# Output product of two gated linear-attention blocks: eight half-size products made seven

## The chip, the cores and the metric

The kernel runs on one core of a Trainium2 chip. The metric is device time in microseconds (us) from one launch; lower is better. Three runs of the kernel before gave 212.53, 211.25 and 210.63 us, a median of 211.25 us. In the views, PE is TensorE's matmul side and PEld its weight load, DVE is VectorE, ACT ScalarE, POOL GpSimd, SP SyncE; a `q` after an engine (SPq) means DMA issues from that engine's queue.

## The reference

Two linear-attention blocks A and B read the same x (2048 rows, 640 columns, bf16). Each has 32 heads of 20 columns, and they are mixed by a gate per row:

```python
def _A_ref(x, wqkv, wo):                      # _B_ref is the same
    qkv = (x @ wqkv) ...                      # q, k, v: 32 heads of 20
    phi = lambda t: jnp.where(t > 0, t + 1, jnp.exp(t)) + 1e-6
    pq, pk = phi(q), phi(k)
    kv = jnp.einsum("bhsd,bhse->bhde", pk, v)
    z = jnp.einsum("bhsd->bhd", pk)
    num = jnp.einsum("bhqd,bhde->bhqe", pq, kv)
    den = jnp.einsum("bhqd,bhd->bhq", pq, z)[..., None] + 1e-6
    return merged_heads(num / den) @ wo
x = A_x
g = _sigmoid((x * gate_w).sum(-1, keepdims=True))
return g * a + (1 - g) * b
```

## The kernel before, in words

Everything is kept transposed so that no activation has to be turned over. For each block b the kernel makes `pqT[b]`, the 640 features of phi(q) on partitions (five chunks `c` of 128) by 2048 rows, scaled in place by gate and 1/den; and `M[b]`, a 640 x 640 matrix that holds kv and wo folded together. The output is then one product over both blocks: out = pqT[A]^T M[A] + pqT[B]^T M[B].

The stages, in the order of the program, are these.

- `k_first` and `k_chunk` (lines 174 to 189): k for 16 row tiles of 128, ten matmuls of 320 columns each; `phi` (166 to 172) is an exp on ScalarE and two instructions on VectorE.
- `q_pass` (386): q in ten units of 1024 columns, with the row sums `z_rows` (235) between the first two. VectorE's `zr` (246) is what the sums go through.
- `g_all` (398): five passes `g_pass` of 32 matmuls (x^T phi(k) for one feature chunk), copied to `GT` by ScalarE (`evac`, 217 to 220). Between them `norm_unit` (312) scales `pqT[b]`.
- `kvt_pass` (263): 30 short matmuls into one PSUM tile, then six masked copies on VectorE into `KVT` (280).
- `m_unit` (287): four matmuls for 128 rows of `M[b]`, then a copy by `evac`.
- The output stage. Row tile i needs 20 matmuls of 320 columns: 2 blocks x 2 column halves x 5 chunks. Tiles 0 and 1 are woven into block B's `kvt_pass` and `m_unit` through `final_mm` (332), so that TensorE has work while `GT`, `KVT` and `M[B]` are copied. Tiles 2 to 14 go through `final_group` (348), tile 15 through `final_last` (360), which splits its columns 448 and 192 so that the last copy and the last DMA are small. Each tile is copied to bf16 by ScalarE or VectorE in turn (`final_out`, 344) and written to memory by SP's queue.

Block B runs after block A; A's `M` units sit among B's k chunks.

Order and waits: a scheduler orders each engine's instructions and adds the semaphore waits. PSUM is eight banks of 512 fp32 columns; `ps` (57) hands out four tiles (slots 0 to 3), each of two banks. Waits are made per tile and not per bank: a writer of one bank of a tile waits for earlier readers of the other bank of that tile.

The block that the change replaces is at lines 450 to 471:

```python
    for c in range(DT):
        m_unit(1, c, ("act", "dve")[c % 2], 1 + c % 2)
        if c > 0:
            for i in range(2):
                final_mm(i, 1, c - 1, pts[i])
```

Of the kernel before, what the change touches and what calls it, by code (L numbers as in the profile page):

```python
# [20 lines left out]
HB = 512  # L21
HF = D // 2
JW = 120
NJ = 6
EPS = 1e-6
RB = 256


@with_exitstack
def kernel(  # L30
# [11 lines left out]
    nc = tc.nc  # L42
# [35 lines left out]
    gwr = persist.tile([P, DT, H], BF16, name="gwr")  # L78
    zero = persist.tile([P, HB], BF16, name="zero")
    grow = persist.tile([1, D], BF16, name="grow")  # L80
    ge = [persist.tile([P, 2 * RB], FP32, name=f"ge{b}") for b in "AB"]

    wq_dram = [A_wqkv.rearrange("(c p) f -> p c f", p=P), B_wqkv.rearrange("(c p) f -> p c f", p=P)]
# [25 lines left out]
    for r in range(4):  # L109
        rows = slice(32 * r, 32 * r + 32)  # L110
# [8 lines left out]
    for r in range(4):  # L119
        rows = slice(32 * r, 32 * r + 32)  # L120
# [96 lines left out]
    def evac(dst, pt, eng):  # L217

        copy = nc.scalar.copy if eng == "act" else nc.vector.tensor_copy
        copy(out=dst.rearrange("p (b n) -> p b n", b=2), in_=pt[:, :, 0:HF])  # L220
# [42 lines left out]
    def kvt_pass(b, slot=None):  # L263

        pt = ps(f"kv{'AB'[b]}", slot)
        for j in range(NJ):
            e0 = JW * j if j < NJ - 1 else D - P
            d0 = JW * j
            w = min(JW, D - d0)
            dst = pt[:, j // 3, (j % 3) * JW:(j % 3) * JW + w]  # L270
            for c in range(DT):
                nc.tensor.matmul(
                    dst, lhsT=wv[b][:, c, e0:e0 + P], rhs=GT[:, c, d0:d0 + w], start=(c == 0), stop=(c == DT - 1),
                )
        for j in range(NJ):
            last = j == NJ - 1
            rows = P if last else JW
            nh = 2 if last else 6
            mask = maskE[:rows, DT - 1, H - 2:H] if last else maskE[:rows, 0, 0:6]
            nc.vector.tensor_tensor(  # L280
                out=KVT[:rows, j, JW * j:JW * j + nh * Dh].rearrange("p (h t) -> p h t", t=Dh),
                in0=pt[:rows, j // 3, (j % 3) * JW:(j % 3) * JW + nh * Dh].rearrange("p (h t) -> p h t", t=Dh),
                in1=mask[:, :, None].to_broadcast([rows, nh, Dh]),
                op=ALU.mult,
            )

    def m_unit(b, c, eng, slot=None):

        pt = ps(f"m{'AB'[b]}", slot)
        for hf in range(2):  # L290
            for k, j in enumerate((c, c + 1)):
                rows = P if j == NJ - 1 else JW
                nc.tensor.matmul(  # L293
                    pt[:, hf, 0:HF], lhsT=KVT[:rows, j, c * P:(c + 1) * P],
                    rhs=wo_sb[b][:rows, j, hf * HF:(hf + 1) * HF], start=(k == 0), stop=(k == 1),
                )
        evac(M[b][:, c, :], pt, eng)

    def rec_pass(b, h, zsel, slot):
# [9 lines left out]
            nc.vector.reciprocal(out=rT[:], in_=d1[:])  # L309
        return rT  # L310

    def norm_unit(b, h, rT, ms, slots):

        pts = [ps(f"ex{'AB'[b]}", s) for s in slots]
        for k, m in enumerate(ms):
            for j in range(4):
                nc.tensor.matmul(
                    pts[j // 2][:, j % 2, k * RB:(k + 1) * RB], lhsT=E4[32 * j:32 * j + 32, m * P:(m + 1) * P],
                    rhs=rT[32 * j:32 * j + 32, :], start=True, stop=True,
                )  # L320
        n = len(ms)
        for jj in range(2):
            src = pts[jj][:, :, 0:n * RB].rearrange("p j (m n) -> p j m n", n=RB)
            r0 = h * 2 * HB + jj * HB
            dst = pqT[b][:, ms[0]:ms[0] + n, r0:r0 + HB].rearrange("p m (j n) -> p j m n", n=RB)
            if jj == 1:
                ex = work.tile([P, 2, n, RB], BF16, tag=f"ex{n}", name="ex")
                nc.scalar.copy(out=ex[:], in_=src)
                src = ex[:]
            nc.vector.tensor_tensor(out=dst, in0=src, in1=dst, op=ALU.mult)  # L330

    def final_mm(i, b, c, pt):
        for hf in range(2):
            nc.tensor.matmul(  # L334
                pt[:, hf, 0:HF], lhsT=pqT[b][:, c, i * P:(i + 1) * P], rhs=M[b][:, c, hf * HF:(hf + 1) * HF],
                start=(b == 0 and c == 0), stop=(b == 1 and c == DT - 1),
            )

    def rows_of(i):
        n, q = divmod(i, CB)  # L340
        rows = out2[n * HB:(n + 1) * HB, :]
        return rows.rearrange("(p q) d -> q p d", q=CB)[q] if n == 0 else rows[q * P:(q + 1) * P, :]

    def final_out(i, pt):
        osb = work.tile([P, D], BF16, tag="osb", name="osb", bufs=3)
        evac(osb[:], pt, ("act", "dve")[i % 2])
        nc.sync.dma_start(out=rows_of(i), in_=osb[:])

    def final_group(i):
        pt = ps("o")  # L350
        for hf in range(2):
            for b in range(2):
                for c in range(DT):
                    nc.tensor.matmul(  # L354
                        pt[:, hf, 0:HF], lhsT=pqT[b][:, c, i * P:(i + 1) * P], rhs=M[b][:, c, hf * HF:(hf + 1) * HF],
                        start=(b == 0 and c == 0), stop=(b == 1 and c == DT - 1),
                    )
        final_out(i, pt)

    def final_last(i):  # L360

        osb = work.tile([P, D], BF16, tag="osb", name="osb", bufs=3)
        for lo, hi, copy, eng in ((0, 448, nc.vector.tensor_copy, nc.sync), (448, D, nc.scalar.copy, nc.scalar)):
            pt = ps("o")
            for k in range(2 * DT):
                b, c = divmod(k, DT)
                nc.tensor.matmul(  # L367
                    pt[:, 0, 0:hi - lo], lhsT=pqT[b][:, c, i * P:(i + 1) * P], rhs=M[b][:, c, lo:hi],
                    start=(k == 0), stop=(k == 2 * DT - 1),
                )  # L370
            copy(out=osb[:, lo:hi], in_=pt[:, 0, 0:hi - lo])
            eng.dma_start(out=rows_of(i)[:, lo:hi], in_=osb[:, lo:hi])

    def load_w(b, which, eng):
        lo = {"q": 0, "k": D, "v": 2 * D}[which]
# [22 lines left out]
    def g_all(b, zsel):  # L398

        units = [(h, ms) for h in range(2) for ms in ((0, 1), (2, 3), (4,))]  # L400
        rts = [rec_pass(b, 0, zsel, 0)]

        def norm():
            h, ms = units.pop(0)
            norm_unit(b, h, rts[h], ms, (2, 3))

        g_pass(b, 0, 1, lambda: rts.append(rec_pass(b, 1, zsel, 2)))
        for c in range(1, DT):
            if c > 1:
# [21 lines left out]
    zsel = q_pass(0)  # L431
    wq[1] = load_w(1, "q", nc.sync)
    g_all(0, zsel)


    turn[0] = 2
# [5 lines left out]
    for i in range(3, ST):  # L442
        k_chunk(1, i)
        if i % 2 == 0 and i // 2 - 2 < DT:
            m_unit(0, i // 2 - 2, "act")
    zsel = q_pass(1)
    g_all(1, zsel)


    pts = [ps("o", 0)]  # L450
    for c in range(DT):
        final_mm(0, 0, c, pts[0])
    kvt_pass(1, 2)
    pts.append(ps("o", 3))
    for c in range(DT):
        final_mm(1, 0, c, pts[1])
    for c in range(DT):
        m_unit(1, c, ("act", "dve")[c % 2], 1 + c % 2)
        if c > 0:
            for i in range(2):  # L460
                final_mm(i, 1, c - 1, pts[i])
    for i in range(2):
        final_mm(i, 1, DT - 1, pts[i])
        final_out(i, pts[i])
    for i, slot in ((2, 1), (3, 2), (4, 0), (5, 3)):
        turn[0] = slot
        final_group(i)
    for i in range(6, ST - 1):
        turn[0] = (1, 2, 0, 3)[(i - 2) % 4]
        final_group(i)  # L470
    final_last(ST - 1)


# [28 lines left out]
```

## Time and profile before

| what | value |
|---|---|
| runs before | 210.63, 211.25, 212.53 us |
| span of the profiled execution (the page gives no other time for it) | 209.1 us |
| TensorE busy | 200.8 us, 96% |
| VectorE, ScalarE busy | 113.7 us (54%), 74.2 us (35%) |
| granted TensorE clock, mean | 1.000 |
| block B's last g matmul is followed by the output stage's first at | 157.69 us |
| last DMA issue (ScalarE's queue, 48 KB) | 206.44 us |

The span runs from the first to the last instruction. A matmul's duration in a row (299 ns for 320 columns) is its way through the array; matmuls overlap, and the distance from start to start is what each costs a busy TensorE. In a timeline line the first two numbers are start and length, and the bracket at the end says how long the engine sat idle before it and what ended that.

### The profile page before, as it was taken

The page shows a single profiled execution, that of the slowest core. Times are in us where ns is not written, and L with a number is a line of the kernel's source. Part 1 is how long each engine was busy: PE and PEld are TensorE (multiplying, and loading weights), DVE is VectorE, ACT ScalarE, POOL GpSimd, SP SyncE. Part 2 cuts the span into 40 slices and gives each one's busy share as a digit, 9 for nine tenths or more (in the row PEclk, how much of TensorE's full clock was granted, in tenths as well). Part 3 has the DMA queues.
Part 4 walks back from the last instruction along what each step waited for, and adds up shares of the span by engine and source line. Part 5 has one row for each costly group of instructions (what it writes and reads, how often), then busy time and mean ns, then how long its engine had stood idle before and what let it go on. Part 6 is the DMA issues. An engine that isn't in the chain of part 4 may idle for free.

```text
span 209.1 us, 3659 instructions
## 1 busy us (share of the span) xinstructions
PE 200.8 (96%) x1561; PEld 126.6 (61%) x1567; DVE 113.7 (54%) x170; ACT 74.2 (35%) x96; POOL 8.6 (4%) x22
## 2 busy tenths in 40 slices
PE   7996989999999999999999999999999999999994
PEld 3674665444466667777764444566667677777762
DVE  3396665867895571677676677957542311111111
ACT  2452545253503452356653435225431331111110
POOL 8800000000000000000000000000000000000000
PEclk9999999999999999999999999999999999999999
DMA  6664499992050000130000000000000011111111
GB/s 202 181 78 101 100 299 365 230 223 94 2 157 3 0 0 3 18 138 3 0 0 3 0 0 0 5 0 0 3 0 3 0 63 67 62 63 63 66 63 63
DMA packets 18015, 14.21 MB, mean 68 GB/s; under 512 B 8863, under 2 KB 17744, under 8 KB 18000
## 3 DMA queue, kind: packets, MB, share of 16 engines
q1 hardware_dynamic: 17422, 13.45, 23.3%
q10 hardware_dynamic: 578, 0.54, 0.8%
q8 instruction: 12, 0.20, 0.4%
q14 instruction: 3, 0.02, 0.0%
HBM read 9.40 MB, written 2.62 MB: 58 GB/s over the span
## 4 chain that ended last, share of the span: by engine, by line
PE 82%; SPq 9%; DMA 3%; DVE 2%; ACT 1%; issue 1%; DVEq 0%; ACTq 0%
PE o L354 17%; PE gB L229 11%; PE gA L229 11%; PE kB L175 10%; PE qA L211 9%; PE qB L211 9%; SPq L103 9%; PE o L334 3%; PE kA L175 2%; DMA wkA<-in_A_wqkv_dram 2%; DMA xT<-in_A_x_dram 1%; PE mA L293 1%; PE o L367 1%; PE mB L293 1%; ACT e L170 1%
## 5 line engine op out<-in xcount | busy, mean ns | idle before, releaser
L175 PEld LDWEIGHTS <-xT 128*128 128x128 bf16 x320 | 30.8, 98 | 15.9 <-DMA xT<-in_A_x_dram 3.4
L229 PEld LDWEIGHTS <-xn 128*128 128x128 bf16 x320 | 29.8, 98 | 14.0 <-issue 2.5
L171 DVE TENSOR_SCALAR e<-e 128x640 bf16<-128x640 bf16 (+1 forms) x52 | 19.4, 374 | 24.6 <-ACT e L170 22.9
L175 PE MATMUL kA<-wkA,xT 128*128 128x320 bf16 x160 | 22.9, 299 | 2.8 <-DMA xT<-in_A_x_dram 2.6
L229 PE MATMUL gB<-pk,xn 128*128 128x320 bf16 x160 | 23.3, 300 | 0.0
L229 PE MATMUL gA<-pk,xn 128*128 128x320 bf16 x160 | 23.3, 300 | 0.0
L175 PE MATMUL kB<-wkB,xT 128*128 128x320 bf16 x160 | 22.9, 299 | 0.0
L354 PE MATMUL o<-MA,pqTA 128*128 128x320 bf16 x130 | 22.1, 299 | 0.0
L354 PE MATMUL o<-MB,pqTB 128*128 128x320 bf16 x130 | 21.9, 299 | 0.0
L211 PE MATMUL qA<-xT,wqA 128*128 128x512 bf16 x97 | 21.8, 379 | 0.1
L211 PE MATMUL qB<-xT,wqB 128*128 128x512 bf16 x97 | 21.8, 379 | 0.1
L220 DVE CAST osb<-o 128x640 bf16<-128x640 f32 x7 | 5.8, 824 | 29.2 <-PE o L354 27.4
L211 PEld LDWEIGHTS <-wqB 128*128 128x128 bf16 x100 | 9.6, 98 | 11.4 <-issue 0.3
L220 ACT CAST osb<-o 128x640 bf16<-128x640 f32 x8 | 5.5, 692 | 31.0 <-PE o L354 30.5
L211 PEld LDWEIGHTS <-wqA 128*128 128x128 bf16 x100 | 9.5, 97 | 11.6 <-issue 0.5
L170 ACT ACTIVATE e<-kA 128x640 bf16<-128x640 f32 x16 | 11.3, 706 | 14.5 <-PE kA L175 14.5
L354 PEld LDWEIGHTS <-pqTB 128*128 128x128 bf16 x130 | 12.7, 98 | 4.9
L354 PEld LDWEIGHTS <-pqTA 128*128 128x128 bf16 x130 | 12.7, 98 | 4.9
L170 ACT ACTIVATE e<-kB 128x640 bf16<-128x640 f32 x16 | 11.3, 704 | 11.7 <-PE kB L175 11.7
L170 ACT ACTIVATE e<-qB 128x1024 bf16<-128x1024 f32 x10 | 10.2, 1024 | 13.4 <-PE qB L211 11.0
L170 ACT ACTIVATE e<-qA 128x1024 bf16<-128x1024 f32 x10 | 10.2, 1024 | 13.1 <-PE qA L211 10.7
L172 DVE SCALAR_TENSOR_TENSOR pk<-kB,e 128x640 bf16<-128x640 f32 x16 | 13.2, 824 | 1.7
(82 smaller groups left out, 172.7 us busy)
## 6 DMA issues: line engine op xcount, KB each, us to landing
out_dram<-osb SPq DMA_DIRECT2D x15, 160.0 KB, 1.8
xn<-in_A_x_dram SPq DMA_DIRECT2D x3, 640.0 KB, 7.6
wqA<-in_A_wqkv_dram SPq DMA_DIRECT2D x1, 800.0 KB, 5.2
wvA<-in_A_wqkv_dram SPq DMA_DIRECT2D x1, 800.0 KB, 12.3
wkB<-in_B_wqkv_dram SPq DMA_DIRECT2D x1, 800.0 KB, 14.0
wqB<-in_B_wqkv_dram SPq DMA_DIRECT2D x1, 800.0 KB, 4.5
wvB<-in_B_wqkv_dram SPq DMA_DIRECT2D x1, 800.0 KB, 4.5
woA<-in_A_wo_dram SPq DMA_DIRECT2D x1, 750.0 KB, 14.6
```

The lines of the kernel that those rows point to most:

```text
L103: nc.sync.dma_start_transpose(out=xT[:, c, n * HB:(n + 1) * HB], in_=x2[n * HB:(n + 1) * HB, c * P:(c + 1) * P])
L170: nc.scalar.activation(out=e[:], in_=src, func=ACT.Exp)
L171: nc.vector.tensor_scalar(e[:], e[:], 1.0, EPS, op0=ALU.min, op1=ALU.add)
L172: nc.vector.scalar_tensor_tensor(out=dst, in0=src, scalar=1.0 + EPS, in1=e[:], op0=ALU.add, op1=ALU.max)
L175: nc.tensor.matmul(pt[:, hf, 0:HF], lhsT=xT[:, c, i * P:(i + 1) * P], rhs=wk[b][:, c, hf * HF:(hf + 1) * HF], start=(c == 0), stop=(c == D ...
L211: nc.tensor.matmul(pt[:, u, :], lhsT=wq[b][:, c, m * P:(m + 1) * P], rhs=xT[:, c, n * HB:(n + 1) * HB], start=(c == 0), stop=(c == DT - 1),)
L220: copy(out=dst.rearrange("p (b n) -> p b n", b=2), in_=pt[:, :, 0:HF])
L229: nc.tensor.matmul(pt[:, hf, 0:HF], lhsT=xn[:, i, c * P:(c + 1) * P], rhs=pk[:, i, hf * HF:(hf + 1) * HF], start=(i == 0), stop=(i == ST - 1),
L293: nc.tensor.matmul(pt[:, hf, 0:HF], lhsT=KVT[:rows, j, c * P:(c + 1) * P], rhs=wo_sb[b][:rows, j, hf * HF:(hf + 1) * HF], start=(k == 0), ...
L334: nc.tensor.matmul(pt[:, hf, 0:HF], lhsT=pqT[b][:, c, i * P:(i + 1) * P], rhs=M[b][:, c, hf * HF:(hf + 1) * HF], start=(b == 0 and c == 0) ...
L354: nc.tensor.matmul(pt[:, hf, 0:HF], lhsT=pqT[b][:, c, i * P:(i + 1) * P], rhs=M[b][:, c, hf * HF:(hf + 1) * HF], start=(b == 0 and c == 0) ...
L367: nc.tensor.matmul(pt[:, 0, 0:hi - lo], lhsT=pqT[b][:, c, i * P:(i + 1) * P], rhs=M[b][:, c, lo:hi], start=(k == 0), stop=(k == 2 * DT - 1),)
```

## The change

The rows are cut in an upper half (tiles 0 to 7) and a lower half (tiles 8 to 15), the output columns in two halves of 320, and the inner dimension in the two blocks A and B. The output is then a product of two 2 x 2 block matrices. It was eight block products; it is now seven, in the variant of Strassen's scheme with shared sums (Winograd's). With a11, a21 the upper and lower rows of pqT[A], a12, a22 those of pqT[B]:

- left operands: s1 = a21 + a22 (overwrites a21), s2 = s1 - a11 and s4 = a12 - s2 (written into `xT`, which is free by then), D3 = a11 - a21 (new tile, made after block A);
- right operands: `TM[0]`, `TM[1]`, `TM[2]`, `TM[3]`, sums of halves of M[A] and M[B], in the buffers of the old k and q weights;
- class `Pair` handles row tiles i and i + 8 together: seven products `p1` to `p7`, each five matmuls of 320 columns (35 for two tiles, 40 before). Products 6, 4 and 3 accumulate in PSUM on product 1, 7 and 5. ScalarE copies p1 and u2 = p1 + p6 to SBUF as fp32; VectorE makes five fp32 additions of 128 x 320 per pair, u3 and the four quarter results.

All operand sums are VectorE instructions: two of 128 x 5 x 512 for D3 after block A, one of 128 x 1600 for TM[0] during block B, three of 128 x 5 x 512 for the first 512 rows at the end of block B, three more in pairs 1, 2 and 3, and 15 of 128 x 320 (`m_sums`) among block B's M units. The M units' copies of block B are all ScalarE's. The output tiles are `oX`, `oW`, `oY`, `oZ`, one slot of two banks each; pair i uses bank i % 2 of all four. Output copies have two buffers for the upper row tile (`osb0`) and two for the lower (`osb1`). The last part of the program keeps the order in which it is written (`manual_schedule`).

In the built program TensorE's order from block B's last g pass on is: p1 of pair 0, kvt, p1 of pair 1, M unit 0, p5 of pair 0, M units 1 and 2, p5 of pair 1, M units 3 and 4, p2 of pairs 0 and 1, then p7, p6 of pair 0, p7, p6 of pair 1, p4, p3 of pair 0, p1, p2 of pair 2, p4, p3 of pair 1; from pair 2 on p7, p6, p5 of pair i, p1, p2 of pair i + 1, p4, p3 of pair i.

```diff
+    def p_diff():
+        for rows in (slice(0, HB), slice(HB, SH)):
+            up = slice(SH + rows.start, SH + rows.stop)
+            add_rows(D3[:, :, rows], pqT[0][:, :, rows], pqT[0][:, :, up], ALU.subtract)
+    def p_sums(rows, ks=(1, 2, 4)):
+        up = slice(SH + rows.start, SH + rows.stop)
+        a11, a21, a12, a22 = [pqT[b][:, :, r] for b in range(2) for r in (rows, up)]
+        s2, s4 = xT[:, :, rows], xT[:, :, up]
+        for k, dst, a, b, op in (
+            (1, a21, a21, a22, ALU.add), (2, s2, a21, a11, ALU.subtract), (4, s4, a12, s2, ALU.subtract)
+        ):
+            if k in ks:
+                add_rows(dst, a, b, op)
+    def m_sums(c):
+        a, b = M[0][:, c, :], M[1][:, c, :]
+        lo, hi = slice(0, HF), slice(HF, D)
+        add_rows(TM[1][:, c, :], b[:, hi], TM[0][:, c, :], ALU.subtract)
+        add_rows(TM[2][:, c, :], b[:, hi], a[:, hi], ALU.subtract)
+        add_rows(TM[3][:, c, :], b[:, lo], TM[1][:, c, :], ALU.subtract)
...
+    def prod(dst, left, right, i, first):
+        r0 = i * P
+        for c in range(DT):
+            nc.tensor.matmul(
+                dst, lhsT=left[:, c, r0:r0 + P], rhs=right[:, c, :], start=(first and c == 0), stop=(c == DT - 1), skip_group_check=not first,
+            )
+    def out_add(dst, acc, sb):
+        nc.vector.tensor_tensor(out=dst, in0=acc, in1=sb, op=ALU.add)
...
+        def at(self, bank):
+            return acc[bank][:, self.i % 2, 0:HF]
+        def p1(self):
+            prod(self.at("x"), pqT[0][:, :, 0:SH], M[0][:, :, 0:HF], self.i, True)
+            self.p1s = work.tile([P, HF], FP32, tag="e", name="p1s", bufs=3)
+            nc.scalar.copy(out=self.p1s[:], in_=self.at("x"))
+        def p2(self):
+            prod(self.at("w"), pqT[1][:, :, 0:SH], M[1][:, :, 0:HF], self.i, True)
+            out_add(self.osb[0][:, 0:HF], self.at("w"), self.p1s[:])
+        def p7(self):
+            prod(self.at("y"), D3, TM[2], self.i, True)
+        def p6(self):
+            prod(self.at("x"), xT[:, :, 0:SH], TM[1], self.i, False)
+            self.u2 = tmp("u2")
+            nc.scalar.copy(out=self.u2[:], in_=self.at("x"))
+            self.u3 = tmp("u3")
+            out_add(self.u3[:], self.at("y"), self.u2[:])
+        def p5(self):
+            prod(self.at("z"), pqT[0][:, :, SH:S], TM[0], self.i, True)
+        def c22(self):
+            out_add(self.osb[1][:, HF:D], self.at("z"), self.u3[:])
+        def p4(self):
+            prod(self.at("y"), pqT[1][:, :, SH:S], TM[3], self.i, False)
+            out_add(self.osb[1][:, 0:HF], self.at("y"), self.u2[:])
+            nc.sync.dma_start(out=rows_of(self.i + ST // 2), in_=self.osb[1][:])
+        def p3(self, last=False):
+            rows = rows_of(self.i)
+            if last:
+                nc.sync.dma_start(out=rows[:, 0:HF], in_=self.osb[0][:, 0:HF])
+            prod(self.at("z"), xT[:, :, SH:S], M[1][:, :, HF:D], self.i, False)
+            out_add(self.osb[0][:, HF:D], self.at("z"), self.u2[:])
+            lo = HF if last else 0
+            nc.sync.dma_start(out=rows[:, lo:D], in_=self.osb[0][:, lo:D])
...
     g_all(0, zsel)
+    p_diff()
...
+    add_rows(TM[0], M[0][:, :, HF:D], M[0][:, :, 0:HF], ALU.subtract)
     g_all(1, zsel)
...
+    with tc.manual_schedule():
+        p_sums(slice(0, HB))
+        half = ST // 2
+        acc = {"x": ps("oX", 0)}
+        pairs = [Pair(i) for i in range(half)]
+        pairs[0].p1()
+        kvt_pass(1, 2)
+        pairs[1].p1()
+        acc["z"] = ps("oZ", 3)
+        for c in range(DT):
+            if c == 1:
+                pairs[0].p5()
+            if c == 3:
+                pairs[1].p5()
+            m_unit(1, c, "act", 1 + c % 2)
+            m_sums(c)
+        acc["w"] = ps("oW", 2)
+        acc["y"] = ps("oY", 1)
+        for p in pairs[0:2]:
+            p.p2()
+        for p in pairs[0:2]:
+            p.p7()
+            p.p6()
+            p.c22()
+        pairs[0].p4()
+        pairs[0].p3()
+        for i in range(1, half):
+            p, after = pairs[i], pairs[i + 1] if i + 1 < half else None
+            if i > 1:
+                p.p7()
+                p.p6()
+                p.p5()
+                p.c22()
+            if after is not None:
+                after.p1()
+                after.p2()
+            p.p4()
+            p.p3(after is None)
+            if i < 4:
+                p_sums(slice(HB, SH), ((1,), (2,), (4,))[i - 1])
```

More of the change, by code (lines that the diff above doesn't have):

```diff
@@ L26 @@
 RB = 256
+SH = S // 2
 @with_exitstack
@@ L80 @@
     grow = persist.tile([1, D], BF16, name="grow")
+    D3 = persist.tile([P, DT, S // 2], BF16, name="D3")
+    TM = [None] * 4
     ge = [persist.tile([P, 2 * RB], FP32, name=f"ge{b}") for b in "AB"]
@@ L310, in rec_pass, with add_rows @@
         return rT
+    def add_rows(dst, a, b, op):
+        nc.vector.tensor_tensor(out=dst, in0=a, in1=b, op=op)
+    def p_diff():
[17 more added lines that the diff above has]
+        add_rows(TM[3][:, c, :], b[:, lo], TM[1][:, c, :], ALU.subtract)
     def norm_unit(b, h, rT, ms, slots):
@@ L330, in norm_unit @@
             nc.vector.tensor_tensor(out=dst, in0=src, in1=dst, op=ALU.mult)
[L332 to L337, printed above, removed]
     def rows_of(i):
@@ L342, in rows_of @@
         return rows.rearrange("(p q) d -> q p d", q=CB)[q] if n == 0 else rows[q * P:(q + 1) * P, :]
[L344 to L372, printed above, removed]
+    def prod(dst, left, right, i, first):
[4 more added lines that the diff above has]
+            )
@@ new lines, in out_add, with tmp, __init__ @@
+    def out_add(dst, acc, sb):
+        nc.vector.tensor_tensor(out=dst, in0=acc, in1=sb, op=ALU.add)
+    def tmp(name):
+        return work.tile([P, HF], FP32, tag=name, name=name)
+    class Pair:
+        def __init__(self, i):
+            self.i = i
+            self.osb = [work.tile([P, D], BF16, tag=f"osb{k}", name=f"osb{k}") for k in range(2)]
+        def at(self, bank):
[31 more added lines that the diff above has]
+            nc.sync.dma_start(out=rows[:, lo:D], in_=self.osb[0][:, lo:D])
@@ L446 @@
     zsel = q_pass(1)
-    g_all(1, zsel)
[L450 to L471, printed above, removed]
+    for tag, ks in (("wk", (0, 3)), ("wq", (1, 2))):
+        t = wpool.tile([P, 2, DT, HF], BF16, tag=tag, name="TM" + tag)
+        for n, k in enumerate(ks):
+            TM[k] = t[:, n]
+    add_rows(TM[0], M[0][:, :, HF:D], M[0][:, :, 0:HF], ALU.subtract)
+    g_all(1, zsel)
+    with tc.manual_schedule():
[38 more added lines that the diff above has]
+                p_sums(slice(HB, SH), ((1,), (2,), (4,))[i - 1])
 _INS = ['A_x', 'A_wqkv', 'A_wo', 'B_x', 'B_wqkv', 'B_wo', 'gate_w']
```

## The prediction

> **What bounds the kernel now.** I read the page first: busy shares, granted clock, chain.
>
> ```profile
> PE 200.8 (96%) x1561; PEld 126.6 (61%) x1567; DVE 113.7 (54%) x170; ACT 74.2 (35%) x96; POOL 8.6 (4%) x22
> ...
> PE 82%; SPq 9%; DMA 3%; DVE 2%; ACT 1%; issue 1%; DVEq 0%; ACTq 0%
> ```
>
> TensorE is the bound, and the chain that ended last is mostly its own. So a matmul taken out is worth its start-to-start distance, as long as no wait takes its place. Next the order of time around the output stage:
>
> ```profile
> 157.69 1.52 PE L334 MATMUL o<-MA,pqTA 128*128 128x320 bf16 x10
> 157.89 0.69 ACT L220 CAST GT<-gB 128x640 bf16<-128x640 f32 x1 [3.49 <-PE gB L229]
> 159.04 1.59 PE L272 MATMUL kvB<-GT,wvB 128*128 128x120 bf16 x30
> 160.49 1.52 PE L334 MATMUL o<-MA,pqTA 128*128 128x320 bf16 x10
> 160.68 1.14 DVE L280 TENSOR_TENSOR KVT<-kvB,maskE 120x120 bf16<-120x120 f32 x6 [5.83 <-PE kvB L272]
> 161.84 1.25 PE L293 MATMUL mB<-woB,KVT 120*128 120x320 bf16 x8
> 162.59 0.69 ACT L220 CAST MB<-mB 128x640 bf16<-128x640 f32 x1 [4.01 <-PE mB L293]
> ...
> 163.33 0.30 PE L334 MATMUL o<-MB,pqTB 128*128 128x320 bf16 x1 [0.24 <-ACT MB L220]
> ```
>
> Ten matmuls take 159.04 - 157.69 = 1.35 us, so 0.136 each and 0.68 for a product of five. Hand-overs show here too. While ScalarE copies the last piece of GT, TensorE has ten matmuls to do. M's first four matmuls end at 161.84 + 0.54 = 162.38 and ScalarE starts 0.20 later; the copy ends 163.28 and TensorE starts 0.05 later, 0.4 us after it could have (eight matmuls from 161.84 end at 162.93).
>
> Then the end of the program and the DMAs:
>
> ```profile
> 205.28 0.62 DVE L371 CAST osb<-o 128x448 bf16<-128x448 f32 x1 [3.78 <-PE o L367]
> ...
> 205.44 0.58 PE L367 MATMUL o<-MB,pqTB 128*128 128x192 bf16 x5
> ...
> 206.09 0.32 ACT L371 CAST osb<-o 128x192 bf16<-128x192 f32 x1 [2.07 <-PE o L367]
> 206.44 0.37 ACTq L372 DMA_DIRECT2D out_dram<-osb  x1
> ```
>
> ```profile
> DMA to landing us min/median/max: 1.5/1.8/2.4
> ```
>
> The last line is of the output's DMAs. VectorE starts 0.25 us after TensorE's group (its successor begins at 205.03). From the last issue to the span's end, 209.1, are 2.66 us. Last, the groups by shape, for durations:
>
> ```profile
> L304 DVE SCALAR_TENSOR_TENSOR d<-denA,geA 128x256 f32<-128x256 f32 x2 | 0.9, 426 | 0.4 <-PE denA L146 0.4
> L246 DVE TENSOR_TENSOR zr<-zB,E 128x640 bf16<-128x640 f32 x1 | 0.8, 814 | 0.0
> L330 DVE TENSOR_TENSOR pqTB<-ex,pqTB 128x1024 bf16<-128x1024 bf16 x4 | 2.8, 689 | 0.2
> L330 DVE TENSOR_TENSOR pqTB<-ex,pqTB 128x512 bf16<-128x512 bf16 x2 | 0.8, 425 | 0.3 <-ACT ex L328 0.3
> L220 ACT CAST osb<-o 128x640 bf16<-128x640 f32 x8 | 5.5, 692 | 31.0 <-PE o L354 30.5 <-PE o L334 0.5
> ```
>
> **Removed.** 40 of 320 output matmuls: 40 x 0.136 = 5.44 us, all on the path. Also before's 0.40 us wait for M, 15 copies of 640 columns and the split of the last tile.
>
> **Prices of what is added.** None of these shapes is in the trace, so each has two ends. An fp32 addition out of PSUM, 128 x 320: between 426 ns (256 columns) and 814 (640); by the line through both 0.49 us. ScalarE's copy of 320: between 319 ns (192 columns, the last copy) and 692 (640); 0.43. A bf16 sum of 320: from 425 at 512 and 689 at 1024 columns (0.516 ns a column), 0.33; of 1600: 0.99; of 2560: 1.48, or 1.72 if 689 is scaled by 2.5. Independent VectorE instructions overlap (the six KVT copies take 1.14 us, though each is 273 ns or 186): 0.08 less from start to start.
>
> **Sums that I cost at nothing.** D3 (2 x 1.48 = 2.96 us) falls where VectorE idles 5.13 us after block A's last scaling. TM[0] (0.99) stands before the phi of B's last k chunk and delays it by about 0.9 us; the row sums that need it come 0.2 us later still. The first-half sums (3 x 1.48 = 4.44) start when the last scaling frees VectorE, 154.1, and with its remaining 0.43 end at 159.3, while the KVT copies can start at 160.07: 0.8 us of cover, hardly any at 1.72 each. The second-half sums lie in pairs 1 to 3, where VectorE then has 5 x 0.49 + 1.48 = 3.9 us of work per pair of 4.76 us on TensorE. If any of these covers is gone, the excess goes straight to TensorE through the copies queued behind.
>
> **Waits added, in order of time** (TensorE starts the stage at 157.69; waits read from the built program):
>
> 1. p1 of pair 0 covers GT's copy with 0.68 us, not 1.35: 0.07; M unit 0 waits for the second KVT copy, 0.09.
> 2. M units 0 to 4 are all copied by ScalarE, 0.69 each. kv ends 159.89, p1 of pair 1 160.56, M unit 0 runs 160.65 to 161.19; with 0.68 a product and 0.54 a unit the others end at 162.42, 162.96, 164.19 and 164.73. The copy of unit 3 ends 165.08, that of unit 4 165.77. p2 of pair 0 needs unit 3's slot (0.40) and, for its last matmul, unit 4's rows (0.15), and ends at 165.96.
> 3. p2 of pair 1 writes bank 1 of oW, but waits for the addition that reads bank 0. On VectorE that one is queued behind 15 `m_sums`, three after each M copy. Three take 0.75 to the next start (3 x 0.33 - 3 x 0.08); unit 4's begin at 165.87 behind unit 3's, so the addition runs 166.62 to 167.11. TensorE stands from 165.96 to 167.16: 1.20. Without any overlap it is 0.85 more (1.08 for three, from 162.1 on).
> 4. p7 of pair 1 waits for u3 of pair 0, for the same reason: 0.20 + 0.43 (ScalarE's u2) + 0.04 + 0.49 + 0.05 = 1.21 after p6, nothing in between.
> 5. p4 of pair 0 waits for u3 of pair 1: again 1.21.
> 6. Pair 2's first addition needs the output buffer of pair 0, whose DMA is issued at 175.15 and lands 1.8 later, at 176.95 (p4 and p3 of pair 0 run 172.98 to 174.34, the addition of p3 to 175.1). Behind it on VectorE is the addition of p4 of pair 1, for which p7 of pair 2 waits: with 0.41 and 0.49 for the two, and 0.05, 177.90 against 177.05: 0.85 (0.55 at a landing of 1.5, 1.45 at 2.4).
> 7. From then on p7 of each pair waits for the addition of p4 of the pair before: 0.25 + 0.49 + 0.05 = 0.79 against 0.68 of p3: 0.12, five times (pairs 3 to 7), 0.6.
> 8. Pair 7 has no successor to put in between: p4 waits 1.20 after p6, of which p5 fills 0.68: 0.52.
>
> Sum 0.07 + 0.09 + 0.55 + 1.20 + 1.21 + 1.21 + 0.85 + 0.6 + 0.52 = 6.3 us.
>
> **The end.** Work from 157.69: 280 x 0.136 = 38.08, kv 1.45, M units 20 x 0.136 = 2.72; with the waits 48.55, so TensorE issues its last at 206.24 (before about 205.85). The last addition starts at 206.50 and ends 206.99; SP, which issues two other DMAs (0.33 each) from 206.3 on, issues at 207.04, against 206.44: 0.6 later. It carries 80 KB (landing between 1.5 for 48 KB and 1.8 for 160), with 240 KB just ahead: 0.2 more. Span 209.1 + 0.8 = 209.9 us. The median of the runs lies 2.15 above the profiled span (the lowest 1.53), so 212.1 us.
>
> In short: 5.44 and 0.40 come off, 6.3 of waits and 0.4 of tail go on.
>
> **Two rules beside the rows.** TensorE's gaps need not slow its clock here: between 18 and 20 us it was busy 0.49 of 2.00 us, the clock row says 1.00, and the 40 matmuls from 20.10 on took 5.61 us, 0.136 each.
> The Trainium skill, "TensorE: Matmul & The Clock Gate", section "A second HAM failure mode: psum-queue depth-cycling", says that frequent small idles between matmul groups make the gate swing to half speed; by that page the 11 products between 166.0 and 177.9 would take twice their time, an estimate of 7.5 us more. The trace so far differs.
> The Trainium skill, "PSUM — Partial Sum Buffer", summary of rules, asks for a guard by bank only; by that the waits 3, 4, 5, 6 and 7 (5.07 us) would not be needed. No row of this trace shows such an access.
>
> **Rivals.**
> Faster: the waits 3 to 7 cost little, because VectorE and ScalarE, 54% and 35% busy, run ahead. Span 209.9 - 5.07 = 204.8, so 207.0 us. Against it: the additions stand in one queue behind things that TensorE itself feeds late.
> Slower, VectorE: no overlap, and 0.60 us an addition (between 0.49 and 0.69, the scaling's row of 128 x 512 out of PSUM). `m_sums` + 0.85, and 0.11 more in waits 3, 4, 5, 8 and the tail, twice in 6, five times in 7: 0.85 + 12 x 0.11 = 2.2. 214.3 us. It decides (over 1%) from about 0.53 us an addition.
> Slower, buffers: the addition of p2 needs the output buffer of two pairs back, whose DMA has from 0.8 to 3.7 us after that pair's p3, 2.9, to land. At 3.2 us: 1.4 in wait 6 and 5 x 0.3 in later pairs, 215.0 us; it decides from 2.95. Against it: 2.4 is the longest here, with a tenth of the DMA time used.
> Slower, clock: 7.5 us more if the gate closed, 219.6; the row above speaks against it.
>
> **How the numbers follow.** Forecast 0.62, faster 0.11, VectorE 0.16, buffers 0.06, clock 0.05. The forecast alone spans 211.0 to 213.5: 0.6 less if wait 7 vanishes and 0.5 less at the short landing, 0.85 more without overlap in 3, 0.6 at the long landing. For 8 in 10 I reach to VectorE's case and half-way towards the faster one: 209.8 to 214.6. A measurement of this kernel tells about 1% from no change: under 209.1 is faster, over 213.4 slower. Faster 0.11; slower 0.24 (the three slower cases, most of them); same 0.65.
>
> **What would show it.** Right: 280 products 0.136 us apart; TensorE idle about 1.2 us three times between 165 and 174 us, ended by VectorE or ScalarE; 0.1 us before most p7; clock 1.00; the last DMA issue about 0.6 us later than before. Wrong: gaps of a few tenths there (faster rival); additions over 0.53 us or VectorE waiting for a DMA in every pair (slower ones); a stall in block B's q pass or before the KVT copies, where I counted none.

## The result and the profile after

The changed kernel takes 212.09 us (median of 20 runs, 211.36 to 213.84); the kernel before, beside it on the same chip, takes 211.37 (20 runs). The ratio is 1.0048, with a 95% interval of 1.0026 to 1.0071 (the two medians alone would give 1.0034): within 1%, as forecast (212.1 us). In 6 of the 20 runs the mean granted clock was 0.992, and these took 212.95 to 213.84 us; the last section comes back to them. The page, with the lines that answer to those of before:

```profile
PE 198.5 (94%) x1527; PEld 122.8 (58%) x1527; DVE 140.7 (66%) x224; ACT 76.3 (36%) x105; POOL 8.6 (4%) x22
...
PEclk9999699999999999999999999999999999999999
...
PE 78%; DMA 6%; SPq 6%; DVE 5%; ACT 2%; issue 1%; DVEq 0%; ACTq 0%
```

VectorE's share went from 54 to 66%, and in the chain TensorE's share fell from 82 to 78%, with VectorE's and the DMAs' grown. The one 6 in the clock row comes before the change and is treated at the end: this profiled execution (time 213.84, span 212.1) lost 1.9 us there, so its output stage begins at 159.55 and not at 157.69. I therefore count inside the stage, from the start of the first output product to the issue of the last store. Before, that is 206.44 - 157.69 = 48.75 us; after, 209.35 - 159.55 = 49.80. So the stage is 1.05 us longer, 0.50% of 211.4, and the times say 0.48%.

The timeline of after, in the same stretch that the prediction went through wait by wait:

```profile
159.55 0.84 PE L372 MATMUL oX<-MA,pqTA 128*128 128x320 bf16 x5
...
165.40 1.26 PE L296 MATMUL mB<-woB,KVT 120*128 120x320 bf16 x8
...
166.88 0.89 PE L372 MATMUL oW<-MB,pqTB 128*128 128x320 bf16 x5 [0.23 <-ACT MB L223]
...
168.28 0.48 DVE L377 TENSOR_TENSOR osb<-oW,p1s 128x320 bf16<-128x320 f32 x1
168.82 0.84 PE L372 MATMUL oW<-MB,pqTB 128*128 128x320 bf16 x5 [1.05 <-DVE osb L377]
...
170.18 0.84 PE L372 MATMUL oX<-TMwq,xT 128*128 128x320 bf16 x5
171.06 0.43 ACT L406 COPY u<-oX 128x320 f32<-128x320 f32 x1 [3.63 <-PE oX L372]
171.51 0.49 DVE L377 TENSOR_TENSOR u<-oY,u 128x320 f32<-128x320 f32 x1 [1.32 <-ACT u L406]
...
172.06 0.84 PE L372 MATMUL oY<-TMwq,D 128*128 128x320 bf16 x5 [1.04 <-DVE u L377]
...
172.73 0.84 PE L372 MATMUL oX<-TMwq,xT 128*128 128x320 bf16 x5
...
174.62 0.84 PE L372 MATMUL oY<-TMwk,pqTB 128*128 128x320 bf16 x5 [1.04 <-DVE u L377]
```

The chain of wait 4 can be read off the rows: p6 of pair 0 starts at 170.18, ScalarE copies from 171.06, VectorE adds from 171.51, and p7 of pair 1 starts at 172.06. Five matmuls at 0.136 end 0.68 after 170.18, so TensorE stands 1.20 us (the bracket is shorter, 1.04, since it starts at the modelled end of the matmul before). By the same count p2 of pair 1 stands 1.21 (the five matmuls ahead of it took 0.73 and not 0.68) and p4 of pair 0, behind the p6 at 172.73, 1.21. In this order, waits 4, 3 and 5, the forecast was 1.21, 1.20 and 1.21.

Further on, the timeline shows the waits behind the output buffers and at the last pair:

```profile
176.69 0.36 SPq L428 DMA_DIRECT2D out_dram<-osb  x1
...
178.01 0.84 PE L372 MATMUL oZ<-MB,xT 128*128 128x320 bf16 x5
...
178.59 0.49 DVE L377 TENSOR_TENSOR osb<-oW,p1s 128x320 bf16<-128x320 f32 x1 [1.92 <-DMA out_dram<-osb]
...
179.53 0.84 PE L372 MATMUL oY<-TMwq,D 128*128 128x320 bf16 x5 [0.68 <-DVE osb L377]
...
185.04 0.33 SPq L428 DMA_DIRECT2D out_dram<-osb  x1
...
188.49 0.84 PE L372 MATMUL oZ<-MB,xT 128*128 128x320 bf16 x5
...
188.95 0.49 DVE L377 TENSOR_TENSOR osb<-oW,p1s 128x320 bf16<-128x320 f32 x1 [1.43 <-DMA out_dram<-osb]
189.89 0.84 PE L372 MATMUL oY<-TMwq,D 128*128 128x320 bf16 x5 [0.55 <-DVE osb L377]
...
207.06 0.84 PE L372 MATMUL oY<-TMwk,pqTB 128*128 128x320 bf16 x5 [0.41 <-DVE u L377]
```

```profile
DMA to landing us min/median/max: 1.7/1.8/4.1
```

Pair 2's first addition waits for the store issued at 176.69, which frees its buffer 1.9 us later, and p7 of that pair stands 0.84 us (forecast 0.85). Pair 4's first addition waits for the store of pair 2 issued at 185.04, which frees its buffer only 3.9 us later, and its p7 stands 0.72. The p7 of pairs 3, 5, 6 and 7 stand 0.06 each, p4 of the last pair 0.57.

The groups by shape, in the output stage of after:

```profile
L377 DVE TENSOR_TENSOR osb<-oZ,u 128x320 bf16<-128x320 f32 x16 | 7.8, 491 | 1.7 <-PE oZ L372 1.1
...
L316 DVE TENSOR_TENSOR xT<-pqTA 128x2560 bf16<-128x2560 bf16 x2 | 3.0, 1482 | 0.0
L316 DVE TENSOR_TENSOR TMwq<-MB,TMwk 128x320 bf16<-128x320 bf16 x5 | 1.6, 323 | 1.5 <-ACT MB L223 1.5
```

An addition takes 0.49 us, a sum of 2560 columns 1.48, one of 320 columns 0.32, ScalarE's copy 0.43 (in the timeline above): the prices that the prediction read off lines between other shapes.

### The profile page after: what moved, and what is told of

The parts are those of the page before. It is cut to its first block, busy times and chain, and to the rows that moved or that the text cites. A ratio compares the mean times of both kernels' runs of the same rounds, so it can differ in the third digit from the quotient of the medians.

```text
span 212.1 us, 3648 instructions
## 1 busy us (share of the span) xinstructions
PE 198.5 (94%) x1527; PEld 122.8 (58%) x1527; DVE 140.7 (66%) x224; ACT 76.3 (36%) x105; POOL 8.6 (4%) x22
## 4 chain that ended last, share of the span: by engine, by line
PE 78%; DMA 6%; SPq 6%; DVE 5%; ACT 2%; issue 1%; DVEq 0%; ACTq 0%
PE gA L232 11%; PE gB L232 11%; PE kB L178 10%; PE qA L214 9%; PE qB L214 9%; SPq L106 6%; PE kA L178 6%; PE oY L372 5%; PE oX L372 4%; PE oZ L372 4%; DMA out_dram<-osb 3%; DMA wkA<-in_A_wqkv_dram 2%; DVE osb L377 2%; DMA xT<-in_A_x_dram 2%; PE oW L372 2%; PE mA L296 1%
## 5 line engine op out<-in xcount | busy, mean ns | idle before, releaser
L178 PEld LDWEIGHTS <-xT 128*128 128x128 bf16 x320 | 31.4, 100 | 17.5 <-DMA xT<-in_A_x_dram 4.2
L178 PE MATMUL kA<-wkA,xT 128*128 128x320 bf16 x160 | 24.6, 312 | 3.4 <-DMA xT<-in_A_x_dram 3.0
L175 DVE SCALAR_TENSOR_TENSOR pk<-kA,e 128x640 bf16<-128x640 f32 x16 | 13.2, 825 | 1.5
L175 DVE SCALAR_TENSOR_TENSOR pqTB<-qB,e 128x1024 bf16<-128x1024 f32 x10 | 12.2, 1219 | 0.9
L175 DVE SCALAR_TENSOR_TENSOR pqTA<-qA,e 128x1024 bf16<-128x1024 f32 x10 | 12.2, 1218 | 0.9
L406 ACT COPY u<-oX 128x320 f32<-128x320 f32 x8 | 3.4, 426 | 25.6 <-PE oX L372 25.6
L372 PEld LDWEIGHTS <-pqTB 128*128 128x128 bf16 x80 | 7.8, 97 | 6.5 <-issue 3.5
L361 DVE TENSOR_TENSOR pqTA<-exA,pqTA 128x1024 bf16<-128x1024 f32 (+1 forms) x6 | 6.3, 1047 | 5.8 <-PE exA L348 5.8
```

The source lines that it names most:

```text
L175: nc.vector.scalar_tensor_tensor(out=dst, in0=src, scalar=1.0 + EPS, in1=e[:], op0=ALU.add, op1=ALU.max)
L178: nc.tensor.matmul(pt[:, hf, 0:HF], lhsT=xT[:, c, i * P:(i + 1) * P], rhs=wk[b][:, c, hf * HF:(hf + 1) * HF], start=(c == 0), stop=(c == D ...
L372: nc.tensor.matmul(dst, lhsT=left[:, c, r0:r0 + P], rhs=right[:, c, :], start=(first and c == 0), stop=(c == DT - 1), skip_group_check=not ...
L406: nc.scalar.copy(out=self.u2[:], in_=self.at("x"))
```

## The experiments

The theory: 5.4 us of products are saved and all of it is given back, most of it in waits of TensorE that exist because a wait is made for a tile of two banks, where the next product writes the other bank. The rivals are an addition chain that costs its time whatever the guard, a bound on VectorE, and the output buffers. In the table, "stage" is the stretch defined above, from one profile each; the ratio is to the kernel before, run beside each on the same chip (211.4 us beside after, 210.8 to 211.0 beside the others).

| kernel | stage, us | ratio to before | 95% interval |
|---|---|---|---|
| before | 48.75 | 1 | |
| after | 49.80 | 1.0048 | 1.0026 to 1.0071 |
| one-bank tiles, all | 44.38 | 0.9832 | 0.9804 to 0.9860 |
| more output buffers | 48.38 | 0.9992 | 0.9972 to 1.0012 |
| dummy addition, behind p3 | 49.93 | 1.0048 | 1.0023 to 1.0074 |
| dummy addition, ahead of p4's | 50.62 | 1.0103 | 1.0072 to 1.0133 |
| one-bank tiles, oW only | 47.94 | 0.9947 | 0.9929 to 0.9965 |
| one-bank tiles, oY only | 46.65 | 0.9883 | 0.9864 to 0.9901 |
| no operand sums | 49.32 | 1.0031 | 1.0011 to 1.0050 |
| last sums behind the addition | 49.07 | 0.9995 | 0.9970 to 1.0020 |
| one-bank tiles, last pair reordered | 43.58 | 0.9763 | 0.9744 to 0.9782 |
| the same, with an eighth product | 48.85 | 1.0017 | 0.9988 to 1.0045 |

Stage and time agree roughly: 1 us in the stage goes with about 0.5% in the ratio, and most kernels keep to that within 0.5 us. The largest difference is that of the first one-bank kernel, 4.37 us shorter than before in the stage and 0.0168 (3.5 us) in the times; four of its six runs had a mean clock of 0.991 or 0.992, as some of after's had, which is at least a part of it.

### One bank to a tile

```
-            return acc[bank][:, self.i % 2, 0:HF]
+            return acc[bank][self.i % 2][:, 0:HF]
...
-        acc = {"x": ps("oX", 0)}
+        acc = {"x": one("oX", "left")}
```

`one` makes two tiles of one bank each; oZ, oW and oY are made in the same way, in the same banks as before. The order of the work stays. (The lines that open and close the memory pools for this are left out here.)

> Only the four product tiles change: each two-bank tile becomes two tiles of one bank, so that a writer of one bank no longer waits for a reader of the other. Instructions and their order on every engine stay as in the changed kernel. Theory (the gain went into waits that the tile-wide guard makes): the waits of p2 of pair 1 (1.20 us), p7 of pair 1 (1.21), p4 of pair 0 (1.21) and before p7 of pairs 3 to 7 go, and the wait for the output buffer is hidden behind them down to about 0.2; 4.9 us less than the changed kernel, about 207.2 us, a ratio to before of 0.980. Rival (the additions and copies of VectorE and ScalarE are themselves what TensorE has to wait for): TensorE meets the same data a moment later, and the time stays within 1 us of 212.1.

Measured: 0.9832, 207.38 us (6 runs). Against after that is 0.0216 of before's time less, with an interval of about 0.0036 either way, 3.8 to 5.3 us. The stage is 5.42 us shorter. The timeline of this kernel, over the products that stood longest in after:

```profile
166.52 1.57 PE L377 MATMUL oW<-MB,pqTB 128*128 128x320 bf16 x10 [0.23 <-ACT MB L228]
...
167.93 0.84 PE L377 MATMUL oY<-TMwq,D 128*128 128x320 bf16 x5
168.61 0.84 PE L377 MATMUL oX<-TMwq,xT 128*128 128x320 bf16 x5
169.28 0.84 PE L377 MATMUL oY<-TMwq,D 128*128 128x320 bf16 x5
...
169.94 0.49 DVE L382 TENSOR_TENSOR u<-oY,u 128x320 f32<-128x320 f32 x1 [1.14 <-ACT u L411]
169.96 0.84 PE L377 MATMUL oX<-TMwq,xT 128*128 128x320 bf16 x5
```

The products follow each other every 0.68 us, while ScalarE and VectorE do the same work as before beside them: the addition at 169.94 reads a bank of oY after p7 of pair 1 has started on the other. So the additions themselves cost next to nothing on the path; the guard over both banks did. Two waits are left behind these products: the 0.57 us of the last pair, and a new one of 0.17 that is not the guard's:

```profile
176.36 1.48 DVE L321 TENSOR_TENSOR pqTA<-pqTA,pqTB 128x2560 bf16<-128x2560 bf16 x1
...
177.44 0.84 PE L377 MATMUL oW<-MB,pqTB 128*128 128x320 bf16 x5
...
177.76 0.48 DVE L382 TENSOR_TENSOR u<-oY,u 128x320 f32<-128x320 f32 x1
178.29 0.84 PE L377 MATMUL oY<-TMwk,pqTB 128*128 128x320 bf16 x5
```

Here an operand sum of 2560 columns holds up the addition that makes u3 of pair 2, and p4, which writes the same bank, starts 0.85 behind the start of a p2 that takes 0.68. Of after's waits 3 to 7, 5.42 us by its trace, and the 0.20 ahead of p1, less this 0.17, 5.45 us are gained, and the stage shows 5.42.

The Trainium skill, "PSUM — Partial Sum Buffer", in its summary of rules, asks for a guard by bank; by that page waits 3 to 7 were not needed, and the run agrees, with 5.42 us in the stage.

### The waits one bank at a time

The same edit for oW alone, and for oY alone:

```
+            if bank == "w":
+                return acc[bank][self.i % 2][:, 0:HF]
             return acc[bank][:, self.i % 2, 0:HF]
```

> As after, but only oW, the bank pair of p2, is split into two tiles of one bank; oX, oY and oZ keep one tile for two banks. Theory (the waits are separate terms): wait 3 alone goes, 1.2 us, the three waits of 0.8 to 1.2 us on oY stay; ratio to before 0.999, 210.9 us where after is 212.1. Rival (one wait covers the next: additions run in their own time, and p2 of pair 1 coming earlier only makes p7 wait longer): no gain, ratio 1.005.

Measured 0.9947; the stage is 1.86 us shorter than after's. The trace shows wait 3 gone (1.21 us), waits 4 to 6 with 1.20, 1.20 and 0.85, and p7 of pair 4 at 0.06 where after's profile has 0.72. So in the stage 1.2 us come from the bank and the rest from a store that landed in time in this execution. By the times the gain is 2.1 us (1.5 to 2.7), more than the 1.2 that I expected. Besides the variable landing there is the clock: none of the six runs here had a mean clock under 0.999, while the six of after at 0.992 lift its mean by about 0.45 us.

> As after, but only oY, the bank pair of p7 and p4, is split into two tiles of one bank. Theory (separate terms): waits 4, 5, 6 and 7 go, measured 1.20 + 1.21 + 0.84 + 0.9 in the trace of after, 4.1 us; wait 3 of 1.2 us ahead of p2 of pair 1 stays; ratio to before 0.985, 208.0 us where after is 212.1. Rival (one wait covers the next): all that the version with every bank split gained comes with oY alone, ratio 0.982; or, if the waits move over to oW's additions, under half of it, 0.996.

Measured 0.9883, a gain of 3.5 us (2.9 to 4.1), where 4.1 was expected; the stage is 3.15 us shorter. Its timeline shows why it isn't 4.1:

```profile
170.85 0.49 DVE L379 TENSOR_TENSOR osb<-oZ,u 128x320 bf16<-128x320 f32 x1
...
171.40 0.84 PE L374 MATMUL oZ<-MB,xT 128*128 128x320 bf16 x5 [0.89 <-DVE osb L379]
```

p3 of pair 0 now stands 1.05 us for the addition of pair 1 that reads the other bank of oZ. In after this wait was hidden behind wait 5. So the terms are nearly separate but not wholly: one wait covered another, which the theory had denied. It is gone in the kernel in which oZ is split as well.

### Output buffers

```
-            self.osb = [work.tile([P, D], BF16, tag=f"osb{k}", name=f"osb{k}") for k in range(2)]
+            self.osb = [t[:, i, :] for t in (xn, pk)]
```

xn and pk are no longer read in this stage, so every pair has rows of its own.

> Only the output copies change: every pair has buffers of its own (rows of x and of phi(k), dead by then) instead of two in turn. Theory: the 0.84 us before p7 of pair 2 goes and so does the 0.55 us before p7 of pair 4, both behind an addition that waits for an output DMA; each shrinks to the 0.06 of the other pairs; 1.2 us less than the changed kernel, 210.9 us. The three waits of about 1.05 us before stay. Rival (waits for buffers only stand in for waits for TensorE's own results): no gain, 212.1 us.

Measured 0.9992: 1.2 us less than after (0.5 to 1.8). In the trace no addition waits for a store, p7 of pairs 2 to 7 stand 0.06 to 0.07 us each, and waits 3, 4, 5 and 8 are unchanged. The stage is 1.42 us shorter: 0.77 at pair 2 and 0.66 at pair 4.

### A second bound on VectorE?

One addition more in each pair, u2 + u2 into a row that nobody reads, at two places:

```
             out_add(self.osb[0][:, HF:D], self.at("z"), self.u2[:])
+            out_add(pk[:, self.i, 0:HF], self.u2[:], self.u2[:])
```

> One more fp32 addition per pair on VectorE (u2 + u2 into a dead tile, not part of the computation), behind the addition of p3: eight of 0.4 to 0.5 us, 3.6 us of VectorE work. Theory: VectorE idles there and nothing that TensorE waits for is behind it within a pair; within 0.4 us of the changed kernel, 212.1 to 212.5 us. Rival (VectorE's total work is the bound of the stage): 3.6 us more, 215.7.

Measured 1.0048, the ratio of after: eight additions cost nothing there that the times show. The stage is 0.13 us longer, which is p7 of pair 4 (0.86 in place of 0.72, a store's landing again).

```
+            out_add(pk[:, self.i, 0:HF], self.u2[:], self.u2[:])
             out_add(self.osb[1][:, 0:HF], self.at("y"), self.u2[:])
```

> The same additional instruction, placed just ahead of the addition of p4, which p7 of the next pair waits for. Theory: VectorE has 0.2 us free there, so about 0.2 us per pair arrive at TensorE in pairs 3 to 7 and 0.4 in pair 2: 1.4 us more than the changed kernel, 213.5 us. Rival (total work): 3.6 us more, as in the run with the addition behind p3; rival (VectorE does not matter): 212.1.

Measured 1.0103: 1.2 us more than after (0.4 to 1.9), 0.82 in the stage. The timeline of this kernel at pair 2, where after had 0.84:

```profile
177.40 0.48 DVE L377 TENSOR_TENSOR pk<-u 128x320 bf16<-128x320 f32 x1
177.80 0.48 DVE L377 TENSOR_TENSOR osb<-oY,u 128x320 bf16<-128x320 f32 x1
...
178.33 0.84 PE L372 MATMUL oY<-TMwq,D 128*128 128x320 bf16 x5 [1.08 <-DVE osb L377]
```

p7 of pair 2 stands 1.24, by the 0.40 that the dummy puts in the queue; that of pairs 3 and 5 to 7 stands 0.24 in place of 0.06. That of pair 4 stands 0.43, less than after's 0.72, since a store lands sooner here. The same instruction is free behind the addition that TensorE waits for, and costs ahead of it. VectorE's order sets the price, not its share of the span.

Then the operand sums of pq left out, all six of 2560 columns; products take operands that are not summed:

> As after, with all operand sums of the pq columns on VectorE during the output products left out (six operations of 128 x 2560, 1.48 us each, 8.9 us of VectorE; the products then take operands that are not summed, so the output isn't the reference's). Theory: they lie in VectorE's idle time and cost nothing on the path beyond the 0.1 us that the mask of KVT waits: 212.0 us, ratio to before 1.004. Rival: VectorE with 66% of the span is a second bound in the output products, where the additions queue behind the sums; then 1 to 4 us go, ratio 0.986 to 1.000.

Measured 1.0031, not to be told from after's 1.0048. The stage is 0.48 us shorter, and 0.48 is what p7 of pair 4 stands less for its store (0.24 against 0.72); every other wait has the same length to 0.01 us. So 8.9 us of VectorE work are free in this kernel, and this stage has no second bound there. (In the one-bank kernel, where the waits that hide them are gone, one of these sums costs the 0.17 us shown above.)

### The queue ahead of wait 3

```
-            m_sums(c)
+            if c < DT - 1:
+                m_sums(c)
...
-        for p in pairs[0:2]:
-            p.p2()
+        pairs[0].p2()
+        m_sums(DT - 1)
+        pairs[1].p2()
```

> As after (two-bank tiles), with one move in VectorE's order: the last unit's three operand sums are issued behind the addition of p2 of pair 0, not ahead of it. Theory (wait 3 has two parts, 0.4 for the queue and 0.8 for addition and guard): p2 of pair 1 waits 0.8 instead of 1.2 us, and p7 of pair 0, which needs the second of the three sums, at most 0.1; together 0.3 us less, 211.8 us, ratio 1.003, which the trace must show, since the times can hardly tell it from 1.005. Rival (the wait is the guard and the addition alone, or M's copy sets it): p2 of pair 1 still waits 1.2 us, ratio 1.005.

The timeline of this kernel:

```profile
165.13 0.89 PE L372 MATMUL oW<-MB,pqTB 128*128 128x320 bf16 x5 [0.23 <-ACT MB L223]
...
166.61 0.84 PE L372 MATMUL oW<-MB,pqTB 128*128 128x320 bf16 x5 [0.58 <-DVE osb L377]
```

From p2 of pair 0 to p2 of pair 1 are 1.48 us, in after 168.82 - 166.88 = 1.94: wait 3 is 0.75 and not 1.21, and p7 of pair 0 isn't late. Both parts of wait 3 are real, 0.46 of queue and 0.75 of addition and guard. The ratio, 0.9995, is 1.1 us (0.4 to 1.8) less than after's, where I had expected 0.3. The stage is 0.73 us shorter: 0.46 of the queue and 0.27 again at pair 4's store (0.45 against 0.72).

### A faster version, and the worth of a product

One-bank tiles, p7, p6 and p5 of the last pair put ahead of p4 and p3 of the pair before, and the last pair's second store issued by ScalarE:

```
-            if i > 1:
+            if 1 < i < half - 1:
...
+            if i == half - 2:
+                after.p7()
+                after.p6()
+                after.p5()
+                after.c22()
             p.p4()
             p.p3(after is None)
...
-            nc.sync.dma_start(out=rows_of(self.i + ST // 2), in_=self.osb[1][:])
+            eng = nc.scalar if self.i == ST // 2 - 1 else nc.sync
+            eng.dma_start(out=rows_of(self.i + ST // 2), in_=self.osb[1][:])
```

> The version with one-bank product tiles, and two more edits at its end: p7, p6 and p5 of the last pair are put ahead of p4 and p3 of the pair before, so that 2.0 us of products (p5, p4, p3) lie between the last p6 and the last p4, and the store of the last pair's second half is issued by ScalarE. Theory: in the profile of the one-bank version the last p4 stands 0.57 us (201.27 against 200.02 + 0.68) for u3 of the same pair, and the last store is issued 0.26 after its addition ended (203.57 against 203.31) because SyncE is still busy with the one ahead. Both go: 0.8 us less than the one-bank version, 206.6 us where before is 211.4, ratio to before 0.979; no stall of TensorE over 0.1 us from p2 of pair 0 on. Rival: the end is set by the stores and their landing, not by the products; then the last issue moves by 0.25 at most, and the ratio stays at 0.982.

Measured 206.07 us (5 runs), 0.9763: faster than both kernels. The stage is 0.80 us shorter than with one-bank tiles alone, as expected; by the times the step is 1.5 us (0.7 to 2.2), of which a part is the clock (one run of five at 0.992 here, four of six there). In the list of waits, which counts only idle time after a matmul's modelled end, one line of TensorE is left from the output stage's start on:

```profile
PE oW L377 <- ACT MB L228: 0.2, 1, 0.2
```

Counted from start to start this is wait 2, 0.41 and 0.04. One stall that I had ruled out stays: p4 of pair 2 stands 0.16 behind the operand sum, as in the one-bank kernel.

And with p5 computed twice in every pair of this version:

```
             prod(self.at("z"), pqT[0][:, :, SH:S], TM[0], self.i, True)
+            prod(self.at("z"), pqT[0][:, :, SH:S], TM[0], self.i, False)
```

> The fastest version so far (one-bank tiles, the last pair's products reordered) with an eighth product put back in each pair: p5 is computed twice into the same bank, 8 x 5 matmuls more (the output then holds p5 twice, so it isn't the reference's). Theory: with the waits gone TensorE is the only bound of this stage, and the removed products are worth what the first term of the sum said: 40 x 0.136 = 5.4 us, from 206.1 to 211.5 us, ratio to before 1.002 (from 0.976). Rival: at least part of the gain comes from additions and copies that took the path and not from the products; then under 4 us, ratio below 0.995.

Measured 1.0017, 0.0254 more (0.022 to 0.029), or 5.4 us (4.6 to 6.1). The stage is 5.27 us longer: 5.44 for the matmuls, less the 0.16 of p4 of pair 2, which stands no longer now that p5 gives the sum more time. Without the waits the removed products are worth their 40 x 0.136 us.

## Why the prediction was right

The forecast's time, 212.1 us, was met. Its steps:

- **Removed products**, 5.44 us: right, 5.27 in the stage when they are put back, and with them a wait of 0.16 goes.
- **Prices**: additions 0.49, copies 0.43, sums 0.32 (forecast 0.33) and 1.48. The rival of a slower VectorE had 0.60 for an addition; its place was right (waiting for an addition's end costs, as the dummy ahead of p4's shows), its price wrong.
- **Sums costed at nothing**: right for this kernel. Leaving six of them out gains nothing that a store's landing doesn't explain; only without the bank waits does one of them cost 0.16 to 0.17. The first-half sums leave VectorE idle for 1.14 us ahead of the KVT copies in after, where the forecast had 0.8 (its own terms, 154.1 + 0.43 + 4.44, end at 158.97 and not at 159.3). The sums ahead of the stage don't delay it either: it starts at 157.78, 157.65 and 158.13 us in three traces that ran at a clock of 1.000 throughout (more buffers, oW only, the fastest), and between 156.71 and 157.96 in the other profiles in which the clock did not fall early, against 157.69 before.
- **Wait 1**, 0.16: not there. In after kv starts 0.68 behind p1, M's first unit 0.68 behind the second p1. Why the copy of GT and the second KVT copy don't hold them up, no run tells.
- **Wait 2**, 0.55: 0.39 for the slot (from the end of the eight matmuls at 165.40, 1.09 later, to 166.88), 0.05 for the last matmul.
- **Waits 3, 4, 5**, 1.20, 1.21, 1.21: 1.21, 1.20, 1.21.
- **Wait 6**, 0.85: 0.84.
- **Wait 7**, five times 0.12: four times 0.06, and 0.72 at pair 4. The term was mis-sized: I had each p7 wait for an addition only, and allowed the late store only in the rival on buffers, for all pairs at once. It is the stores of one pair in eight; in the kernels that keep the two buffers and oY's tile of two banks, p7 of pair 4 stands 0.24 to 0.86 us in five profiles and 0.06 in one. This part of that rival was true: the buffer came free after 3.9 us, above the 2.95 from which the rival decides. Not in the list were 0.04 us, five times, ahead of p1 of pairs 3 to 7, on oX's other bank.
- **Wait 8**, 0.52: 0.57.
- **Sum of the waits**, 6.3: 0.39 + 0.05 + 1.21 + 1.20 + 1.21 + 0.84 + 0.96 + 0.20 + 0.57 = 6.6. Errors of both signs, none over 0.4.
- **The end**, 0.6 later: the last issue comes 1.05 later in the stage; of the 0.45 over, 0.3 are the longer sum of the waits, and most of the rest is SP's queue, which issues 0.25 after the last addition's end (209.10 to 209.35) where I had 0.05. From the last issue to the end of the span are 2.75 us (2.66 before), 0.1 and not 0.2 more.

The faster rival, 207.0 us, is what one-bank tiles give, 207.4. Its reason was wrong for after (VectorE doesn't run ahead of the guard), and its 5.07 us right for a kernel without it. The clock rival fell: between 167.7 and 178.0 us TensorE is busy 7.17 of 10.30 us, in gaps of about 1 us, and the granted clock stays at 1.00 (row in the last section).

Pair 2's stores are late for a reason that the traces point at. The DMA view of after from 184.3 to 186 us, with the two stores issued there (the last number is the median of their landings), has one packet of 0.02 MB on a queue that the profile marks as instruction:

```profile
q8 instruction: 1, 0.02, 6.7%
...
out_dram<-osb SPq DMA_DIRECT2D x2, 160.0 KB, 3.9
```

In all twelve profiles the output stores on record that take over 1.9 us (up to 4.2; in before the one of 2.4 at 176.88) are in flight together with such a packet, and no other store takes as long. What is not settled is whether the packet causes the delay and why the delay is 0.2 us in one execution and 2.5 in another: I ran nothing that moves it.

## What to carry to other kernels

Price a cut in TensorE's work together with the hand-overs that it adds: here seven products for eight were worth 5.4 us and were eaten by 6.6 us of waits, 5.6 of them ahead of products that wrote one bank of a tile while only the other was still being read. When banks alternate, give each bank its own tile before judging the scheme. And what an instruction on a half-idle engine costs is decided by its place in the queue: an addition ahead of the one that TensorE waits for cost 0.2 to 0.4 us each time, the same one behind it nothing.

## What the runs showed of the hardware

The granted clock fell early in after's profiled execution. The columns of these windows are the stretch, its length, busy time of TensorE, weight load, VectorE, ScalarE and GpSimd, then the granted clock, the DMA share and GB/s:

```profile
18.00:20.00 2.00, 0.72 (x3) 0.19 (x2) 1.65 (x3) 0.57 (x1) 0.00 (x0) 1.00 0.51 115
20.00:22.00 2.00, 0.32 (x2) 0.21 (x3) 0.00 (x0) 0.00 (x0) 0.00 (x0) 0.84 0.39 83
22.00:24.00 2.00, 2.00 (x9) 1.13 (x8) 0.00 (x0) 0.51 (x1) 0.00 (x0) 0.50 0.56 125
24.00:26.00 2.00, 2.00 (x13) 1.33 (x12) 1.15 (x2) 0.64 (x2) 0.00 (x0) 0.81 0.34 75
...
167.70:178.00 10.30, 7.17 (x51) 4.87 (x50) 4.51 (x11) 1.28 (x3) 0.00 (x0) 1.00 0.08 31
```

TensorE, waiting for x's transposing DMAs, was busy 1.04 of 4 us, its longest idle stretch 1.72 us; then the clock was at half for 3.4 us ((0.16 + 0.50 + 0.19) x 2 / 0.5), just when work came back (9 matmuls in 2 us at 0.50, where before's trace has 17 at 1.00). Before's profiled execution was busy 0.49 of 2 us in the same place and 1.90 in the next 2, and kept its clock. It is a neighbour of the change and no part of it: the edit changes nothing in that stretch, the one-bank kernel's profile shows it too (0.66 and 0.50 between 21 and 25 us), the fastest version's doesn't, and of the 63 runs of before beside the experiments 9 had a mean clock of 0.992 or less as well. It costs 1.9 us in this profile. By the times it is about 1.5: the six runs of after with a mean clock of 0.992 took 213.4 on average, the other 14 211.9. So it adds to the scatter of all these times.

The Trainium skill, "TensorE: Matmul & The Clock Gate", section "HAM oscillation — how this bites in real kernels", tells of gaps over about 3.4 us as the danger. Here the clock fell after a longest gap of 1.72 us, in a stretch of 4 us that was 26% busy, while gaps of about 1 us in a stretch that was 70% busy left it alone.
